# Where the last group step hands over to the first expert block: routing steps and two sums move behind the first block's preparation

## The chip, the cores and the metric

The kernel runs on one core of a Trainium2 chip. The metric is the device time of one execution in microseconds (us): the median of three runs for each kernel. One more execution was recorded by the hardware profiler, and all rows below are from that one.

The engines named here: PE is TensorE (matrix multiplies), DVE is VectorE, ACT is ScalarE, POOL is GpSimd (here mostly a scatterer of rows), and SP is SyncE, which issues most of the transfers. Each engine takes its instructions in the order in which the program wrote them.

## What is computed

First a long convolution per channel by a Fourier transform, then a mixture of experts with two levels of routing, each token going to one of 16 experts:

```
def reference(**kwargs):
    x = _attn_ref(x, h).reshape(8 * 5056, 128)   # irfft(rfft(x) * rfft(h)), 8 batches
    return _moe_ref(x, ...)

def _moe_ref(x, w_group, w_expert, w1, w2):      # 40448 tokens, 128 features
    g_idx = argmax(x @ w_group); g_w = softmax(x @ w_group)[g_idx]       # 4 groups
    e_idx = argmax(x @ w_expert[g]); e_w = softmax(...)[e_idx]           # 4 experts in each
    out[token] = g_w * e_w * (relu(x @ w1[g, e]) @ w2[g, e])             # 128 -> 1024 -> 128
```

## The kernel before

**Rounds.** The convolution is done in three rounds `r` of three sequences each (round 0: the filter and two batches). A round has `stage1(r)`, which transforms along one axis into the tile `st`; then `groups(r)`, which takes the 79 frequencies as 40 pairs `p` (`NQ` is 40; the last pair holds one frequency); then `side(r)`, which finishes the inverse transform, computes the routing of each unit of tokens and scatters the token rows, sorted by expert, into a table in memory (`srt`). `side(r)` runs beside the next round's work, and `side(1)` ends, with its eighth unit, at the place that is changed here. After round 2's groups come the expert blocks `j` of 512 tokens each; `side(2)` runs beside them.

**A group step** `step(k)` (L635) handles two pairs, `k` and `k+1`. It is a generator in eleven parts. In order: the forward transform of pair `k` on PE, its products `y` and `m` on DVE (L540), the same for pair `k+1`; then for both pairs the sum `y += m` (`add`, L572 to L576, on DVE in rounds 1 and 2), with one scatter sent between (`send`); then the inverse transforms on PE of the two pairs before, `k-2` and `k-1` (`inverse`, L578), each followed by a copy `zs` on ACT (L600, or L598 once the experts have begun) and a scatter sent by ACT. So the last full step, `k = 38`, sums pairs 38 and 39 and inverts 36 and 37. Pairs 38 and 39 are inverted by one more step, `k = 40`, whose eleven parts are the list `rest = late(2)` and are woven between the first expert steps, four parts ahead of each: part 1 stores pairs 36 and 37, part 3 inverts pair 38, part 4 pair 39, part 8 stores both. Parts 0 to 3 come ahead of the first expert step, part 4 ahead of the second.

**The hand-over.** After step 38 the entry `turn` (L1625) closes the PSUM pool of the groups (`pp`, three tiles of two banks, used in turn) and opens the experts' pool over the same banks (`pz`, `ptr1`, `px` twice, `ptr0`, `aux`; in this order, so `ptr0` and `aux` lie on the third pair of banks). Then `ffn_first(0)` (L1472) prepares block 0: `ffn_prep_x` transposes the token rows on PE into `ptr0` (L1306), copies ids on DVE (L1307, L1308), and splits x into a high part on ACT (`x0h`, L1298) and a low part on DVE (`x0l`, L1299); `ffn_prep_w` splits two quarters of the weights the same way (`w0h`, `w0l`, `w2h`, `w2l`).

**Expert steps.** A block has eight steps (`ffn_steps`, L1478). Step `i` does three matmuls of the first layer (`mm1`, L1351 to L1353) into one of three banks in turn, then ACT's `h..h` (L1356) and DVE's `h..l` (L1357), and from step 2 the second layer's three matmuls for step `i-2` (`mm2`, L1369 to L1371). Step 0 of block 0 also prepares `w1`, step 2 `w3`. From the fourth step on, a chain of small DVE instructions, `table_a`, computes which experts the blocks from 4 on take (L1097 and what follows); near its start stands one matmul (L1014, in `nblocks`) that needs the DVE instructions ahead of it and waits on PE in the order of the program.

**The routing steps.** Each unit of `side(1)` has 41 small steps, `gate_math` (L879), numbered 0 to 40 here, of which some are empty. Those that matter: 19 to 23 write weights and ids to the rows; 24 to 31 are empty; 32 is four small matmuls (L972, L973) into the bank that `routed()` gives, which is a tile of the groups' pool until the experts begin and the separate bank `py0` after that; 33 is `off` and `base` on DVE (L976, L977), 34 and 35 are `cs` (L979, L981), 36 and 37 `posf` (L984, L986); then a last step puts the unit's 15 scatters into the queue `sends`. `send` takes one scatter from the queue if there is one: DVE or ACT casts one column of positions (L854) and POOL issues the scatter (L855). What is left of the queue is sent at once at `drain`, after expert step 15. The load of block 4's rows (`ffn_x`, L1254 on SP) waits for all of these scatters.

**What sets the order.** All of this is one list `main` of (weight, function), and `weave` (L176) runs the side's steps between its entries:

```
        s["acc"] += w / s["len"]
        while s["done"] < len(s["steps"]) and (s["sacc"] < s["acc"] * s["total"] - 1e-6 or i == s["end"] - 1):
            sw, sf, small = s["steps"][s["done"]]
            if small and room[i + 1] > 0 and i < s["end"] - 1:
                light.append(sf)
            else:
                if small:
                    flush(len(light))
                sf()
```

A side step becomes due when the weights of the entries so far have reached its share. A small one (all of `gate_math`) is put in a waiting list, and the list is spread evenly over the run of entries of weight 0 that follows (`room` counts them; `if w == 0: flush(-(-len(light) // room[i]))`). In a group step the parts 6 and 10 weigh 2.0 and the others 0 (`GW`).

Of the kernel before, what the change touches and what calls it, by code (L numbers as in the profile page):

```python
# [44 lines left out]
NROW = 4  # L45
GW = [0, 0, 0, 0, 0, 0, 2.0, 0, 0, 0, 2.0]
FW = [0, 0, 1.0, 0, 0, 0, 1.0, 0]
W_S1, W_END = 0.45, 2.5
SIDE0, SIDE1, SIDE2 = 10, 14, 24
SLOTS = 56  # L50
LATE = 4
# [25 lines left out]
NQ = (NG + 1) // 2  # L77
# [153 lines left out]
class Kernel:  # L231
# [233 lines left out]
    def groups(self, r):  # L465
# [7 lines left out]
        w = nu * D  # L473
# [15 lines left out]
        def load_h(p):  # L489
            if p >= NQ:  # L490
                return
            ht = cx.tile([128, 3, D], F32, name="hg", bufs=3)
            if r > 0:
                nc.sync.dma_start(out=ht[:, 1:3], in_=self.hd[p])
            hgs[p] = ht

        def negate(p):
            if p < NQ:
                minus[p] = cx.tile([128, 128], F32, name="ns", bufs=2)
                nc.scalar.mul(out=minus[p], in_=cgs[p][:, 128:256], mul=-1.0)  # L500
# [113 lines left out]
        def loads(n):  # L614
            while asked[0] < n:
                load(asked[0])
                asked[0] += 1

        def limit(n):
            return min(n, max(n - 2, last_x + 2)) if r > 0 else n  # L620
# [14 lines left out]
        def step(k):  # L635


            last = [p for p in (k - 4, k - 3) if 0 <= p < NQ and r > 0]
            yield
            if k < NQ:  # L640
                self.beside = "groups"
            elif r < 2:
                self.beside = ""
            loads(limit(k + ahead + 1))
            load_h(k + 2)
            if k == 0:
                negate(0)
                negate(1)
            for p in (k, k + 1):
                if p < NQ:  # L650
                    yield from product(p)
                    if r == 0:
                        nc.sync.dma_start(out=self.hd[p], in_=hgs[p][:, 1:3])
                if p == k:
                    loads(limit(k + ahead + 2))
                    for q in last:
                        store(q)
            for p in (k, k + 1):
                if p < NQ:
                    add(p)  # L660
                    if p == k:
                        self.send()
            yield
            load_h(k + 3)
            back = [p for p in (k - 2, k - 1) if 0 <= p < NQ]
            for i in range(2):
                negate(k + 2 + i)
                if k - 2 + i in back:
                    yield
                    inverse(k - 2 + i)  # L670
                    if r == 2 or i == 1:
                        self.send("s")
            yield
            for _ in range(3 if k >= NQ else 0):
                yield
            if k >= NQ or r == 0:
                for p in back:
                    store(p)
            yield
# [921 lines left out]
    def run(self):  # L1601
        tc = self.tc
        with ExitStack() as ctx:
            self.pools(ctx)
            with ExitStack() as c2:
# [10 lines left out]
                def add(f, w=0.0):  # L1616
                    main.append((w, f))
# [17 lines left out]
                for r in range(3):  # L1635
                    if r == 1:
                        add(self.share)
                    pre, steps = gr[r]
                    rest = late(r - 1) if r > 0 else []
                    n = len(s1[r][1])  # L1640
                    t0 = self.table_0()
                    for k, f in enumerate(s1[r][1]):
                        add(f, W_S1)
                        if r > 0 and k % 2 == 1:
                            add(self.send)
                        if r == 0:
                            add(advance(more))
                        if r == 2 and ("end", 0) in mark:
                            add(advance(t0))
                        if k >= 1:  # L1650
                            for g in rest[RP * k - RP:RP * k]:
                                add(g)
                        if k == SIDE0 and r > 0:
                            add(side[r - 1][0])
                        if k == max(SIDE0 + SIDEG, END0 if r == 2 else 0) and r > 0:
                            mark["start", r - 1] = len(main)
                            if r == 2:
                                mark["end", 0] = len(main)
                        if k >= n - PRE and (k - n) % 5 == 0:
                            add(advance(pre))  # L1660
                    if r > 0:
                        add(lambda: None, W_END)
                    for p in range(0, NQ, 2):
                        for w, f in steps[p // 2]:
                            add(f, w)
                        if p >= NQ - LOAD1:
                            add(advance(s1[r + 1][0] if r < 2 else early))
                add(turn)
                add(lambda: self.ffn_first(0))
                rest = late(2)  # L1670
                ta, tq, tb, fill = self.table_a(), self.table_c(), self.table_b(), self.fill_rows()
                ahead = self.ffn_ahead()
# [69 lines left out]
```

## Time and profile before

| what | us |
|---|---|
| median of three runs | 1768.18 |
| lowest and highest of the three | 1767.53, 1774.45 |
| the profiled execution | 1765.39 |
| its span, first to last instruction | 1763.7 |

The profiled execution lies 2.79 us under the median, and 1.69 us of it lie outside its span. All places in this document are us from the start of that span. A busy time is the time in which an engine had at least one instruction running. In a line of a timeline the first number is the start and the second the time that the instructions took; DVE and ACT overlap the end of one with the start of the next, so that the distance of two starts is shorter than a duration. The brackets at the end give the idle time ahead of the line and what ended it.

### The profile page before, as it was taken

To read this page: it belongs to the slowest core of one execution; us is meant where nothing else is said; L and a number is where in the kernel's file an instruction comes from. 1 tells how busy PE (TensorE), PEld (TensorE's weight loads), DVE (VectorE), ACT (ScalarE), POOL (GpSimd) and SP (SyncE) were. 2 spreads that over 40 slices of the span, in tenths; PEclk is the share of its full clock that TensorE was granted. 3 is DMA by queue.
4 is the path that set the end of the run, shared out by engine and by line. 5 is a ranking of instruction groups with operands and counts; after the bars stand their busy time and mean duration, and the time that the engine had idled before them with its cause. 6 is when DMAs were issued, how large, how long until landed. Compare 5 with 4: busy or idle time off the path is not lost. (4 is left out here: it accounts for less than half of the span.)

```text
span 1763.7 us, 49283 instructions
## 1 busy us (share of the span) xinstructions
PE 1664.1 (94%) x17293; PEld 1289.9 (73%) x17293; DVE 1300.6 (74%) x3092; ACT 1041.4 (59%) x2461; POOL 769.3 (44%) x742
## 2 busy tenths in 40 slices
PE   8998899988898998999999999999999999999997
PEld 7676755557655556777777888787787877888986
DVE  6554598865487787777777778877787777877875
ACT  4564444434434445666666667676667666666765
POOL 1452233342355454144454445254555554334444
PEclk9999999999999999999999999999999999999998
DMA  7797578876578777655665555457545584444554
GB/s 204 217 294 222 163 237 250 263 224 182 167 228 256 252 229 213 175 161 166 172 176 165 165 150 152 126 158 234 161 147 157 170 248 140 130 130 145 156 163 144
DMA packets 281642, 330.30 MB, mean 187 GB/s; under 512 B 33335, under 2 KB 216000, under 8 KB 281368
## 3 DMA queue, kind: packets, MB, share of 16 engines
q1 hardware_dynamic: 252504, 271.00, 52.0%
q0 software_dynamic: 20608, 41.79, 6.9%
q10 hardware_dynamic: 8256, 14.10, 2.8%
q8 instruction: 143, 2.34, 0.6%
q14 instruction: 131, 1.07, 0.2%
HBM read 230.41 MB, written 96.86 MB: 186 GB/s over the span
## 5 line engine op out<-in xcount | busy, mean ns | idle before, releaser
L855 POOL DMA_INDIRECT srt<-rw,pos x320 | 345.8, 1081 | 446.7 <-DVE pos L854 129.3
L1422 POOL DMA_INDIRECT out<-orow,at x176 | 182.0, 1034 | 258.3 <-ACT at L1420 202.4
L540 DVE TENSOR_TENSOR y<-pp,hg 128x768 f32<-128x768 f32 (+1 forms) x120 | 103.6, 863 | 75.6 <-ACT hg L530 31.3
L1422 POOL DMA_INDIRECT out<-orow,sids x92 | 93.7, 1018 | 120.1 <-DVE orow L1389 86.8
L600 ACT COPY zs<-pp 128x768 f32<-128x768 f32 (+1 forms) x118 | 85.2, 722 | 85.9 <-PE pp L590 40.3
L590 PE MATMUL pp<-y,cg 64*64 64x384 f32 (+1 forms) x1472 | 117.2, 442 | 14.4 <-DVE m L540 11.1
L440 DVE TENSOR_TENSOR st<-pp,odd 128x320 f32<-128x320 f32 x96 | 46.9, 488 | 100.7 <-ACT odd L439 94.6
L522 PE MATMUL pp<-st,cg 64*64 64x192 f32 (+1 forms) x1556 | 116.9, 403 | 1.1 <-issue 1.1
L722 PE MATMUL py<-ig,zm 126*64 126x79 f32 x2048 | 93.7, 241 | 20.7 <-issue 14.0
L1357 DVE SCALAR_TENSOR_TENSOR h0l<-px,h0h 128x512 fp32r<-128x512 f32 (+1 forms) x109 | 73.5, 674 | 51.9 <-ACT h0h L1356 33.1
L722 PEld LDWEIGHTS py<-ig,zm 126*64 126x64 f32 x2048 | 80.6, 141 | 41.1 <-issue 29.0
L1356 ACT ACTIVATE h0h<-px 128x512 fp32r<-128x512 f32 (+1 forms) x109 | 63.9, 586 | 75.7 <-PE px L1353 47.7
L743 ACT COPY yT<-py 128x474 f32<-128x474 f32 (+1 forms) x96 | 44.6, 513 | 105.8 <-PE py L736 88.3
L540 DVE TENSOR_TENSOR m<-pp,hg 128x768 f32<-128x768 f32 (+1 forms) x120 | 102.8, 857 | 0.2
L1357 DVE SCALAR_TENSOR_TENSOR h2l<-px,h2h 128x512 fp32r<-128x512 f32 (+1 forms) x112 | 75.4, 673 | 34.8 <-ACT h2h L1356 25.2
L590 PEld LDWEIGHTS pp<-y,cg 64*64 64x64 f32 x1472 | 57.2, 133 | 53.9 <-issue 25.1
L1357 DVE SCALAR_TENSOR_TENSOR h3l<-px,h3h 128x512 fp32r<-128x512 f32 (+1 forms) x111 | 74.5, 671 | 29.3 <-ACT h3h L1356 27.2
L522 PEld LDWEIGHTS pp<-st,cg 64*64 64x64 f32 x1556 | 62.3, 133 | 39.7 <-issue 34.7
L1356 ACT ACTIVATE h3h<-px 128x512 fp32r<-128x512 f32 (+1 forms) x111 | 65.2, 587 | 37.9 <-PE px L1353 26.2
L574 POOL TENSOR_TENSOR y<-y,m 128x512 f32<-128x512 f32 x40 | 50.9, 1276 | 78.5 <-DVE m L562 46.1
L1357 DVE SCALAR_TENSOR_TENSOR h1l<-px,h1h 128x512 fp32r<-128x512 f32 (+1 forms) x111 | 74.6, 672 | 10.5 <-ACT h1h L1356 4.7
L1356 ACT ACTIVATE h1h<-px 128x512 fp32r<-128x512 f32 (+1 forms) x111 | 65.1, 587 | 24.2 <-PE px L1353 10.5
(476 smaller groups left out, 5184.6 us busy)
## 6 DMA issues: line engine op xcount, KB each, us to landing
wr<-in_moe_w SPq DMA_DIRECT2D x373, 256.0 KB
zd<-zs SPq DMA_DIRECT2D x78, 384.0 KB
zm<-zd SPq DMA_DIRECT2D x64, 378.0 KB
cg<-in_c_g SPq DMA_DIRECT2D x102, 224.0 KB
xr<-srt SPq DMA_DIRECT2D x71, 260.0 KB
hg<-hd SPq DMA_DIRECT2D x80, 128.0 KB
zd<-zs SPq DMA_DIRECT2D x39, 256.0 KB
xt<-in_x ACTq DMA_DIRECT2D x54, 160.0 KB
```

Of the source, the lines that this page charges most:

```text
L440: nc.vector.tensor_tensor(out=all_st[:, 0:2 * HALF, d], in0=even, in1=odd, op=ALU.add)
L522: nc.tensor.matmul(px[c * 64:c * 64 + 64, b, to], lhsT=k, rhs=data[:, of], start=begin, stop=i == len(steps) - 1 or p == 0 and i == 1, til ...
L540: nc.vector.tensor_tensor(out=t[:, :, 0:w].rearrange("p t (r u d) -> p t r u d", r=2, u=nu), in0=taken(px, part).unsqueeze(1).broadcast_to ...
L574: (nc.gpsimd if r == 0 else nc.vector).tensor_tensor(out=y[:, :, 0:w], in0=y[:, :, 0:w], in1=m[:, :, 0:w], op=ALU.add)
L590: nc.tensor.matmul(pz[c][h:h + 64, 0:w], lhsT=wt[c * 64:c * 64 + 64, k + h:k + h + 64], rhs=y[c * 64:c * 64 + 64, part, 0:w], start=part = ...
L600: nc.scalar.copy(out=z[:, 0:n, 0:w], in_=pp[:, 0:n, 0:w])
L722: nc.tensor.matmul(pys[q][c:c + 64, col(n, u)], lhsT=zms[q][:, n % QB, k:k + 64], rhs=self.ig[:, 0:NH], start=n % QB == 0 and u == 0, stop ...
L743: nc.scalar.copy(out=self.yT[:, k:k + QB * c1], in_=pys.pop(q)[:, 0:QB * c1])
L855: ins = self.nc.gpsimd.indirect_dma_start(out=self.srt, out_offset=bass.IndirectOffsetOnAxis(ap=k["pos"][0:p, j:j + 1], axis=0), in_=k["rw ...
L1356: nc.scalar.activation(out=hh, in_=p, func=AF.Relu)
L1357: nc.vector.scalar_tensor_tensor(out=hl, in0=p, scalar=0.0, in1=hh.bitcast(F32), op0=ALU.max, op1=ALU.subtract)
L1422: ins = self.nc.gpsimd.indirect_dma_start(out=self.a["out"], out_offset=bass.IndirectOffsetOnAxis(ap=ids, axis=0), in_=o, in_offset=None, ...
```

## The change

Three edits, all of which act in round 2 alone. The `add` of step 38 is left out, and with it the scatter that was sent there; step 40 now does both sums, in its part 1, which stands behind `ffn_first(0)`. The eleven parts of step 38 get the weight 1e-6 in place of 2.0 or 0. `ffn_first(0)` gets the weight that they had together, 4.0.

```
+W_S1, W_END, QUIET = 0.45, 2.5, 1e-6
             for p in (k, k + 1):
-                if p < NQ:
+                if p < NQ and (r < 2 or k < NQ - 2):
                     add(p)
                     if p == k:
                         self.send()
+                elif r == 2 and p >= NQ:
+                    add(p - 2)
             yield
...
                         for w, f in steps[p // 2]:
-                            add(f, w)
+                            add(f, w if r < 2 or p < NQ - 2 else QUIET)
...
                 add(turn)
-                add(lambda: self.ffn_first(0))
+                add(lambda: self.ffn_first(0), sum(GW))
```

## Rows read from the trace of the kernel before

**Rows 1.** The page, busy time and share of the span of two engines, and instructions.

```profile
PE 1664.1 (94%) x17293; PEld 1289.9 (73%) x17293; DVE 1300.6 (74%) x3092; ACT 1041.4 (59%) x2461; POOL 769.3 (44%) x742
```

**Rows 2.** Stretches of the hand-over: length, then busy us (and instructions) of PE, PE's weight loads, DVE, ACT and POOL, the granted clock of TensorE as a share of 2.4 GHz, the share of the transfer engines, GB/s.

```profile
662.00:669.00 7.00, 2.42 (x27) 1.13 (x24) 6.72 (x19) 2.01 (x5) 4.29 (x4) 1.00 0.72 210
669.00:678.00 9.00, 7.98 (x45) 4.37 (x44) 6.93 (x18) 6.71 (x17) 5.76 (x6) 1.00 0.85 259
678.00:695.00 17.00, 16.51 (x78) 13.20 (x78) 15.13 (x51) 10.98 (x26) 6.89 (x8) 1.00 0.65 171
```

**Rows 3.** The timeline of PE at the hand-over: the inverse of pair 37, the routing matmul, the transposes of block 0, the inverse of pair 38 (first matmul), the first expert step, the inverse of pair 39, the second expert step, the third (first matmul), and the matmul of `table_a`.

```profile
664.79 1.52 PE L590 MATMUL pp<-y,cg 64*64 64x384 f32 x16 [2.48 <-DVE m L540]
666.50 0.18 PE L972 MATMUL pp<-tot,ltri 128*128 128x16 bf16 x1 [0.18 <-DVE m L540]
...
668.67 0.63 PE L1306 MATMUL ptr<-ident,xr 128*128 128x128 f32 x4 [1.92 <-DVE base L977]
669.23 0.53 PE L590 MATMUL pz<-y,xt 64*64 64x384 f32 x1
...
670.68 0.50 PE L1351 MATMUL px<-x0h,w0h 128*128 128x512 f32 x1
671.49 0.50 PE L1352 MATMUL px<-x0h,w0l 128*128 128x512 f32 x1 [0.31 <-DVE w0l L1299]
...
672.15 1.51 PE L590 MATMUL pz<-y,xt 64*64 64x384 f32 x8
673.59 0.50 PE L1351 MATMUL aux<-x0h,w0h 128*128 128x512 f32 x1
...
674.39 0.40 PE L1351 MATMUL px<-x0h,w0h 128*128 128x512 f32 x1
...
678.11 0.17 PE L1014 MATMUL py<-nba_m,ones 128*128 128x16 bf16 x1 [0.82 <-DVE cnta L1099]
```

**Rows 4.** The timeline of DVE at the hand-over (of the two sums the first; the second, and one cast, stand between it and `off`).

```profile
665.49 0.95 DVE L540 TENSOR_TENSOR m<-pp,hg 128x768 f32<-128x768 f32 x1
666.35 0.95 DVE L574 TENSOR_TENSOR y<-y,m 128x768 f32<-128x768 f32 x1
...
668.15 0.17 DVE L976 TENSOR_TENSOR off<-pp,base 128x16 f32<-128x16 f32 x1
668.35 0.17 DVE L977 TENSOR_TENSOR base<-pp,base 128x16 f32<-128x16 f32 x1
...
670.01 0.38 DVE L1307 CAST ids<-xr 128x4 int32<-128x4 f32 x1
...
670.15 0.68 DVE L1299 TENSOR_TENSOR x0l<-ptr,x0h 128x512 fp32r<-128x512 f32 x1
...
671.35 0.68 DVE L1299 TENSOR_TENSOR w2l<-xt,w2h 128x512 fp32r<-128x512 f32 x1
672.89 0.69 DVE L1357 SCALAR_TENSOR_TENSOR h0l<-px,h0h 128x512 fp32r<-128x512 f32 x1 [0.85 <-ACT h0h L1356]
673.50 0.68 DVE L1299 TENSOR_TENSOR w1l<-xt,w1h 128x512 fp32r<-128x512 f32 x1
675.22 0.69 DVE L1357 SCALAR_TENSOR_TENSOR h1l<-aux,h1h 128x512 fp32r<-128x512 f32 x1 [1.04 <-ACT h1h L1356]
...
677.12 0.17 DVE L1097 TENSOR_TENSOR cnta<-base,base 128x16 f32<-128x16 f32 x1
```

**Rows 5.** The timeline of ACT at the hand-over: the copy of pair 37, the high part of x (no instruction stands between the two), and the first `h`.

```profile
666.42 0.80 ACT L600 COPY zs<-pp 128x768 f32<-128x768 f32 x1 [1.73 <-issue]
669.38 0.58 ACT L1298 CAST x0h<-ptr 128x512 fp32r<-128x512 f32 x1 [2.17 <-PE ptr L1306]
...
672.26 0.60 ACT L1356 ACTIVATE h0h<-px 128x512 fp32r<-128x512 f32 x1 [0.41 <-PE px L1353]
```

**Rows 6.** Two places where TensorE's granted clock fell, each with the idle stretch ahead of it and the stretch at the lower clock, and the two idle stretches of the hand-over. Columns as in the second group.

```profile
357.00:359.60 2.60, 0.00 (x0) 0.00 (x0) 2.57 (x7) 0.59 (x3) 1.34 (x2) 1.00 0.99 329
359.60:363.00 3.40, 3.37 (x48) 3.16 (x52) 0.59 (x6) 1.88 (x5) 1.64 (x2) 0.50 0.99 341
...
1250.40:1252.50 2.10, 0.05 (x2) 0.04 (x1) 0.54 (x1) 1.16 (x4) 0.00 (x0) 1.00 0.45 156
...
1253.90:1257.30 3.40, 3.40 (x10) 2.64 (x9) 2.19 (x6) 1.67 (x5) 2.09 (x2) 0.50 0.10 39
...
662.30:664.80 2.50, 0.02 (x2) 0.04 (x1) 2.42 (x8) 0.92 (x3) 1.53 (x2) 1.00 0.30 98
...
666.30:668.60 2.30, 0.27 (x7) 0.17 (x4) 2.27 (x7) 0.80 (x1) 1.49 (x2) 1.00 0.86 262
```

**Rows 7.** The drain and what waits for it: DVE's casts, the first and the last of POOL's four scatters, SP's load of block 4's rows, PE's transposes of these rows.

```profile
701.71 0.33 DVE L854 CAST pos<-posf 128x1 int32<-128x1 f32 x4
702.49 0.69 DVE L1357 SCALAR_TENSOR_TENSOR h0l<-aux,h0h 128x512 fp32r<-128x512 f32 x1 [0.45 <-issue]
...
702.13 0.98 POOL L855 DMA_INDIRECT srt<-rw,pos  x1 [4.23 <-DVE pos L854]
...
706.22 1.17 POOL L855 DMA_INDIRECT srt<-rw,pos  x1 [0.31 <-issue]
...
709.22 0.37 SPq L1254 DMA_DIRECT2D xr<-srt  x1
...
727.85 0.60 PE L1306 MATMUL ptr<-ident,xr 128*128 128x128 f32 x4
```

More of the change, by code (lines that the diff above doesn't have):

```diff
@@ L47 @@
 FW = [0, 0, 1.0, 0, 0, 0, 1.0, 0]
-W_S1, W_END = 0.45, 2.5
+W_S1, W_END, QUIET = 0.45, 2.5, 1e-6
 SIDE0, SIDE1, SIDE2 = 10, 14, 24
```

## The prediction, made before the changed kernel ran

> **What bounds the kernel now.** The page first: PE is busy 94% of the span and no other engine comes near [rows 1], so a change is worth what it takes from PE's idle time or adds to it. The place is the hand-over from the groups to the experts; the stretches around it show where PE's idle time lies. From 662 to 669 PE works 2.42 of 7 us while DVE works 6.72: that stretch is DVE's. From 669 to 678 PE works 7.98 of 9, and from 678 on 16.51 of 17 [rows 2]. So whatever moves the start of the busy stretch moves the end of the kernel by as much, and all that can be won here is the idle time of these 16 us, 5.6 us, or 3.2 us of it behind the inverse of pair 37, ahead of which nothing is moved that takes time. The timeline of PE names the waits behind it: 0.18, 1.92, 0.31 and 0.82 us [rows 3], 3.2 us in all. The largest, 1.92 us, is the transposes of block 0 waiting for `base`: the routing matmuls of the last unit take the third pair of PSUM banks, on which `ptr0` lies after `turn`, and DVE reads them only behind the two sums [rows 3, 4].
>
> **What moves.** I followed the weights through the list by hand. The last group step now has no entry of weight 0, so routing steps 19 to 27, which were spread up to the middle of that step, all come just ahead of it; 24 to 27 are empty, and of the others only 22 and 23 (0.1 to 0.2 us of DVE) pass from inside the step to its front, which shifts nothing behind pair 38's products. Steps 28 to 40 become due behind `ffn_first(0)` and are spread over the entries from `late` part 0 on: the four routing matmuls (32) land ahead of expert step 0, in bank `py0`; `off` and `base` behind expert step 0, the two `cs` and the two `posf` between it and expert step 1. The 15 scatters enter the queue behind the send of expert step 1. The two sums land in `late` part 1, behind block 0's low parts and ahead of the inverse of pair 38.
>
> **Step 1, the front: a gain of 2.07 us at the transposes.** Without the routing matmuls the third pair of banks is free when `m` of pair 39 ends, at 665.49 + 0.95 = 666.44; with the 0.15 us that lay between the end of `base` (668.52) and the transposes, they start at 666.6 in place of 668.67 [rows 3, 4]. The wait may be for the whole pool and so for the copy of pair 37, which ends at 667.22 [rows 5]: then 667.4. I take 666.6, since the wait of before also ended with one tile of that pair of banks; the other end, 0.8 us later, is kept for the range. `x0h` followed the start of the transposes by 0.71 us and `x0l` can follow `x0h` by 0.65: `x0h` 667.3, `x0l` 668.0, in place of 670.15 [rows 4, 5].
>
> **Step 2, what takes the place of the wait.** DVE takes its instructions in order, and behind `m` of pair 39 now stand the ids, `x0l`, `w0l`, `w2l`, and only then the sums. DVE idles from 666.6 to 668.0, where before it did the sums. `w2l` starts 1.20 us behind `x0l` and the next instruction could start 0.60 later: 669.8. The sums start there, the first ends after 0.95, at 670.75 (both took 1.8 us to the next instruction, 666.35 to 668.15 [rows 4], so they are over at 671.6), and the inverse of pair 38 starts at 670.9, in place of 669.23: 1.65 us late. PE idles from 667.2, where the transposes end, to 670.9: 3.7 us.
>
> **Step 3, expert step 0.** The inverse of pair 38 takes 1.45 us from start to next start (669.23 to 670.68), to 672.35. The routing matmuls add some 0.1. The first layer's three matmuls no longer wait for `w0l` (0.31 us): at 0.27 us each (673.59 to 674.39 for three) they run 672.45 to 673.25, and the last ends some 0.1 later [rows 3]. ACT has pair 38's two copies behind the inverse, over at about 673.3; so `h0h` starts at about 673.4, in place of 672.26, and `h0l`, which came 0.63 us later, at 674.0, in place of 672.89 [rows 4, 5]: 1.1 us late.
>
> **Step 4, the routing steps in the experts' way.** Behind `h0l` stand `w1l` (0.61 us later) and now the six routing instructions, which took from 668.15 to 670.01, 1.86 us [rows 4]. `w1l` starts at 674.6, the routing at 675.2, `h1l` at 677.1 in place of 675.22: 1.9 us late. Before, DVE idled 1.04 us ahead of `h1l`, so it is not all new time. PE does not mind at once: the inverse of pair 39 and expert steps 1 to 3 fill it to about 678.2. But `table_a`'s matmul L1014 stands in PE's order, its DVE instructions stand behind `h1l`, `h2l` and `w3l`, and it came 2.89 us behind the start of `h1l` [rows 3, 4]. It now comes at 680.0 in place of 678.11. Nothing behind it in the 17 us that follow has more than 0.5 us of idle time on PE [rows 2], so the 1.9 us stay.
>
> **Step 5, the scatters.** Before, the 15 scatters of the last unit went out at the two late inverses, at expert steps 0, 1, 2, 7, 8, 9 and 10 and at two stores in block 1, 11 in all, and 4 at the drain [rows 7]. Now the queue is empty at the first four of these places (before, ACT already found it empty at the inverse of pair 37: nothing stands between that copy and `x0h` [rows 5]; the send that is left out was the one that it can now use). So the drain has 8. DVE pays four more casts, some 0.33 us, against 0.45 us of idle time behind the four of before. POOL pays 4 x 1.36 us (706.22 - 702.13 over three), 5.5 us, and SP's load of block 4's rows, with block 4's weights behind it and then the next reads of the convolution's result, goes from 709.2 to 716.6 (5.5 and the 1.9 of above). PE wants those rows at 727.85 [rows 7], now 729.7: 13 us are left for the transfer. I cost it at nothing.
>
> **The clock.** Two rows show TensorE's clock falling from 2.4 to 1.2 GHz behind an idle stretch: after 2.6 us without a matmul at 357, and after 2.1 us at 1250.4; each time the lower clock held for the 3.4 us that the row covers. But 2.5 us of idle time at 662.3 and 2.3 us with little work at 666.3 passed at 2.4 GHz [rows 6], so idle time of this length goes either way. The 3.7 us of step 2 are longer than any of these, and follow close on 662.3's. The price: work of 3.4 us at half speed is 1.7 us late; what counts is only the part ahead of expert step 0's `h0h`, 670.9 to 673.3, for DVE has slack behind it. If the fall comes as PE resumes, the 2.4 us of work lose all 1.7; if it comes 1.4 us later, as it did at 1253.9 behind the matmuls that resumed at 1252.5, they lose 1.0 [rows 6]. The Trainium skill (TensorE: Matmul & The Clock Gate, section "Why this matters for your kernels") tells to keep idle gaps out from between bursts of matmuls, since such a gap brings TensorE back to the lower clock; this trace agrees at 357 and not at 662.3. By that rule the clock falls for certain; by the rows alone it is likely.
>
> **The sum.** Gained: nothing that lasts. Lost: 1.9 us by steps 2 to 4, and 1.0 to 1.7 us if the clock falls; I take 1.0, since the rows have falls that came later than the first matmul. 1765.39 + 2.9 = 1768.3 us for a profiled execution, and 1768.18 + 2.9 = 1771.1 us on the median, 0.16%. A measurement of this kernel can tell some 0.5%, 9 us, from no change: this is the same within it.
>
> **The rivals.**
> *The late steps without the clock* (0.25): all of the above and no fall: 1770.1.
> *It does what it looks like* (0.20): PE starts block 0 two us sooner and the sums and routing hide beside PE. For it: DVE idled 0.85 us ahead of `h0l` and 1.04 ahead of `h1l` [rows 4], room for the 1.86 us of routing. Against it: DVE's order puts the sums behind `x0h`'s round trip, and the inverse of pair 38 stands ahead of expert step 0 on PE. At best all 3.2 us of waits go: 1765.0; if step 2 alone fails, some 1768, no change at all.
> *The drain decides, clearly slower* (0.05): block 4's rows, loaded from 716.6, reach PE after 729.7, and PE waits. No row here shows how long this load takes; of before it can be said that it took no more than 727.85 - 709.22 = 18.6 us, since PE has no wait there [rows 7]. It decides from a load of 13.1 us on; with one of 18.6 PE waits 5.5 us: 1768.18 + 1.9 + 5.5 = 1775.6, and with a fall of the clock at its highest price 1777.3, which is beyond the 0.5%. Against it: block 4's weights come behind it in the same queue and were in time too, and a load of 260 KB (512 rows of 130 numbers) is 1.5 us even at the 171 GB/s that all transfers had behind 678 [rows 2].
>
> **Chances and range.** The forecast with the fall has 0.46, with 1771.1 to 1772.6 as its own range (a fall at 1.7 us and the 0.8 us of step 1 on top); the rest as given, and 0.04 for what I have not seen that makes it faster by over 0.5%. The three cases within 0.5% have 0.91 together, slower 0.05, faster 0.04. The three runs of before lie from 0.65 under their median to 6.27 above, and the profiled execution 2.79 under it, so a median can move by 2 to 4 us by itself: from 1765.0, the best of the gains, to 1776, the forecast with most of that spread on top.
>
> **What the profile would show.** Right: transposes at about 666.6 (step 1); sums behind `w2l` and the inverse of pair 38 near 670.9 (step 2); `h0l` near 674.0 (step 3); six routing instructions between `w1l` and `h1l` and L1014 near 680 (step 4; half to one and a half us later with a fallen clock); 8 casts at the drain, and the load of block 4's rows near 716 to 717 with no wait on PE for it (step 5); and a granted clock of 0.5 between 669 and 675. Wrong: the inverse of pair 38 before 669.5, L1014 before 678, or a wait of PE's past 690 that the trace of before does not have.

## The result, and the profile after

The changed kernel is slower: a median of 1783.26 us over 8 runs against 1771.68 for the kernel before in 8 runs beside it, a ratio of 1.0067 with an interval of 1.0046 to 1.0088. The forecast was 1771.1, no change within 0.5%; of the 12.2 us between it and the measured median 3.5 are the kernel before's own, which took 1768.18 then. The profiled execution took 1793.08 us, with a span of 1791.4, 27.7 us more than the profiled one of before. That is more than the medians differ. 10.8 us of it lie ahead of the changed place, in code that the two kernels share (`m` of pair 39 starts at 676.25 in place of 665.49), where the clock fell oftener in this execution (mean granted clock 0.977 over the span, 0.990 in that of before). They are left aside. Places are therefore given from the start of that `m`, and three stretches are compared:

| stretch | before | after |
|---|---|---|
| `m` of pair 39 to `table_a`'s matmul (the hand-over) | 12.62 | 19.18 |
| `table_a`'s matmul to the transposes of block 4's rows | 49.74 | 57.21 |
| from there to the start of PE's last matmul | 1029.55 | 1032.45 |

So the changed kernel loses 6.6 us at the hand-over and 7.5 us in the stretch with the drain. The last row differs by up to 6.6 us among the runs of one sitting below, whose code is the same there (1029.91 to 1036.49 in the third), so its 2.9 us are not put down to the change. Lines of the code after are two higher than before (L1306 is L1308, L1014 is L1016).

PE's timeline at the hand-over after, which answers to [rows 3]:

```profile
678.02 0.66 PE L1308 MATMUL ptr<-ident,xr 128*128 128x128 f32 x4 [0.95 <-ACT zs L600]
682.19 0.90 PE L590 MATMUL pz<-y,xt 64*64 64x384 f32 x1 [3.51 <-DVE y L574]
...
685.10 0.77 PE L1353 MATMUL px<-x0h,w0h 128*128 128x512 f32 x1
...
686.65 2.83 PE L590 MATMUL pz<-y,xt 64*64 64x384 f32 x8
689.41 0.79 PE L1353 MATMUL aux<-x0h,w0h 128*128 128x512 f32 x1
...
695.43 0.18 PE L1016 MATMUL py<-nba_m,ones 128*128 128x16 bf16 x1
```

The transposes come 1.78 us behind `m`, where they came 3.18 behind it. The inverse of pair 38 comes 5.94 behind it, where it came 3.74, and PE is idle for 3.51 us ahead of it. The durations show the rest: 2.83 us for the inverse of pair 39 against 1.51, 0.77 for a first-layer matmul against 0.50. PE runs at half its clock, as three stretches of after show (columns as in [rows 2]):

```profile
678.70:681.10 2.40, 0.00 (x0) 0.00 (x0) 1.72 (x3) 1.62 (x3) 1.18 (x2) 1.00 0.76 217
681.10:694.80 13.70, 12.61 (x44) 6.74 (x45) 7.33 (x17) 4.24 (x9) 0.96 (x1) 0.50 0.47 144
694.80:706.00 11.20, 10.83 (x50) 8.23 (x49) 9.67 (x37) 7.22 (x16) 2.32 (x3) 1.00 0.67 194
```

It stays at 1.2 GHz for 13.7 us. The longest that [rows 6] showed was 3.4. PE is idle only in the first 1.1 of the 13.7 us, ahead of the inverse of pair 38; behind that the profile shows it busy without a pause:

```profile
682.20:694.80 12.60, 12.60 (x44) 6.73 (x45) 6.24 (x15) 4.24 (x9) 0.96 (x1) 0.50 0.44 136
```

DVE's timeline after, which answers to [rows 4]:

```profile
679.38 0.69 DVE L1301 TENSOR_TENSOR x0l<-ptr,x0h 128x512 fp32r<-128x512 f32 x1 [1.80 <-issue]
...
680.59 0.69 DVE L1301 TENSOR_TENSOR w2l<-xt,w2h 128x512 fp32r<-128x512 f32 x1
681.19 1.82 DVE L574 TENSOR_TENSOR y<-y,m 128x768 f32<-128x768 f32 x2
687.39 0.69 DVE L1359 SCALAR_TENSOR_TENSOR h0l<-px,h0h 128x512 fp32r<-128x512 f32 x1 [4.38 <-ACT h0h L1358]
688.00 0.68 DVE L1301 TENSOR_TENSOR w1l<-xt,w1h 128x512 fp32r<-128x512 f32 x1
688.60 0.17 DVE L978 TENSOR_TENSOR off<-py,base 128x16 f32<-128x16 f32 x1
...
690.36 0.17 DVE L988 TENSOR_TENSOR posf<-posf,sg 128x15 f32<-128x15 f32 x1
691.72 0.69 DVE L1359 SCALAR_TENSOR_TENSOR h1l<-aux,h1h 128x512 fp32r<-128x512 f32 x1 [1.18 <-ACT h1h L1358]
```

The order is the predicted one. But DVE still waits 1.18 us for `h1h` behind the six routing instructions: with the clock low they cost nothing, and PE is what is late.

The drain after, which answers to [rows 7]: DVE's casts, POOL's first and last scatter, SP's load of block 4's rows, PE's transposes of these rows.

```profile
719.16 0.57 DVE L856 CAST pos<-posf 128x1 int32<-128x1 f32 x8
...
719.58 0.98 POOL L857 DMA_INDIRECT srt<-rw,pos  x1 [4.51 <-DVE pos L856]
...
728.92 1.01 POOL L857 DMA_INDIRECT srt<-rw,pos  x1 [0.31 <-issue]
...
731.45 0.37 SPq L1256 DMA_DIRECT2D xr<-srt  x1
...
752.64 0.60 PE L1308 MATMUL ptr<-ident,xr 128*128 128x128 f32 x4
```

PE does not wait for these rows. But what PE does while POOL scatters is another matter. `side(2)` gives PE, now and then, a lump of 72 small matmuls (48 of L724, 24 of L738; L722 and L736 before). PE's timeline of the one beside the drain, after:

```profile
722.58 1.73 PE L724 MATMUL py<-ig,zm 126*64 126x79 f32 x44
724.64 0.38 PE L724 MATMUL py<-ig,zm 126*64 126x79 f32 x4 [0.33 <-issue]
725.40 0.50 PE L738 MATMUL py<-igt,zt 64*64 64x158 f32 x5 [0.37 <-issue]
726.83 0.54 PE L738 MATMUL py<-igt,zt 64*64 64x158 f32 x5 [0.94 <-issue]
728.28 0.50 PE L738 MATMUL py<-igt,zt 64*64 64x158 f32 x5 [0.91 <-issue]
729.72 1.16 PE L738 MATMUL py<-igt,zt 64*64 64x158 f32 x5 [0.94 <-issue]
731.17 0.81 PE L738 MATMUL py<-igt,zt 64*64 64x158 f32 x4 [0.29 <-issue]
```

The same lump in before, with two scatters beside it, and the next one, with none:

```profile
705.15 1.85 PE L722 MATMUL py<-ig,zm 126*64 126x79 f32 x47
707.22 0.23 PE L722 MATMUL py<-ig,zm 126*64 126x79 f32 x1 [0.21 <-issue]
707.38 1.62 PE L736 MATMUL py<-igt,zt 64*64 64x158 f32 x24
...
736.06 1.86 PE L722 MATMUL py<-ig,zm 126*64 126x79 f32 x48
737.85 1.04 PE L736 MATMUL py<-igt,zt 64*64 64x158 f32 x24
```

Of these three the one with no scatter takes 2.83 us, the one with two 3.85 and the one with six 9.39. In the last, PE stops after the first 44 matmuls and then after every four or five, for 0.3 to 0.9 us, and waits for nothing that the profile names. Two scatters have no fixed price: other lumps of before with two beside them took 2.83 to 6.15 us. Meanwhile the transfer engines are at 16% and DVE works 1.29 of 9.5 us, so neither looks like the bound (the last four columns are the busy POOL, the clock, the transfer share and GB/s):

```profile
722.50:732.00 9.50, 5.72 (x74) 3.47 (x74) 1.29 (x2) 1.14 (x3) 5.91 (x6) 0.84 0.16 50
728.90:735.70 6.80, 5.70 (x20) 3.85 (x21) 1.39 (x2) 1.77 (x4) 1.43 (x2) 0.50 0.43 130
```

At 728.9 the clock falls once more, for 6.8 us. The lump is 5.5 us longer than that of before; the other 2 of the 7.5 us are put down to this low clock, which no run shows apart from a long lump.

### The profile page after: what moved, and what is told of

The parts are those of the page before. It is cut to its first block, busy times and chain, and to the rows that moved or that the text cites. A ratio compares the mean times of both kernels' runs of the same rounds, so it can differ in the third digit from the quotient of the medians.

```text
span 1791.4 us, 49283 instructions
## 1 busy us (share of the span) xinstructions
PE 1682.0 (94%) x17293; PEld 1297.5 (72%) x17293; DVE 1303.5 (73%) x3095; ACT 1042.9 (58%) x2458; POOL 767.5 (43%) x742
## 5 line engine op out<-in xcount | busy, mean ns | idle before, releaser
L724 PE MATMUL py<-ig,zm 126*64 126x79 f32 x2048 | 92.0, 238 | 20.0 <-issue 14.2
L724 PEld LDWEIGHTS py<-ig,zm 126*64 126x64 f32 x2048 | 79.4, 139 | 41.5 <-issue 29.6
L1359 DVE SCALAR_TENSOR_TENSOR h1l<-px,h1h 128x512 fp32r<-128x512 f32 (+1 forms) x111 | 74.7, 673 | 16.2 <-ACT h1h L1358 11.6
```

What stands on the lines that cost most here:

```text
L724: nc.tensor.matmul(pys[q][c:c + 64, col(n, u)], lhsT=zms[q][:, n % QB, k:k + 64], rhs=self.ig[:, 0:NH], start=n % QB == 0 and u == 0, stop ...
L1359: nc.vector.scalar_tensor_tensor(out=hl, in0=p, scalar=0.0, in1=hh.bitcast(F32), op0=ALU.max, op1=ALU.subtract)
```

## The experiments

The experiments ran in four sittings, each beside the kernel before on the same chip. In the first two the kernel before took 1697.48 and 1694.32 us, in the others 1772.79 and 1758.43. One chip served in the second and in the last, so this is no property of a chip. In the first two, the short sittings, the lump at the drain takes 2.83 us (in one run 3.00) with two or three scatters beside it, but for the run in which it was moved. The page's group of L722 shows the difference over the whole kernel, in before and, below it, in the kernel before of the second sitting (busy time, mean ns, idle time ahead and what ended most of it):

```profile
L722 PE MATMUL py<-ig,zm 126*64 126x79 f32 x2048 | 93.7, 241 | 20.7 <-issue 14.0
```

```profile
L722 PE MATMUL py<-ig,zm 126*64 126x79 f32 x2048 | 82.6, 236 | 9.4 <-ACT rw L780 5.4
```

The 14.0 us of idle time without a named releaser no longer lead. So the short sittings show the hand-over alone, the long ones both costs.

**The first sitting: one part at a time.** Sums put back in the changed kernel (weights kept):

```
-                if p < NQ and (r < 2 or k < NQ - 2):
+                if p < NQ:
                     add(p)
...
-                elif r == 2 and p >= NQ:
-                    add(p - 2)
```

> The changed kernel with its first edit undone: the sums of pairs 38 and 39 and the scatter between them are back in the last group step; the weights stay, so the routing steps stay behind block 0's preparation. From the start of pair 39's product m to table_a's matmul it was 12.62 us before and 19.18 after; from that matmul to block 4's transposes 49.74 before and 57.21 after. Theory (PE's idle gap in front of the inverse of pair 38 lets the clock fall, and apart from that the doubled drain holds up the side's matmuls): the first stretch comes back to 11.5 to 14 us with no fall of the clock in it, the second stays long, 54 to 58 us, since the drain still has 8 scatters. Rival (the routing steps between h0l and h1l are what costs): the first stretch stays at 16 us or more.

The second is the kernel before with this edit the other way round. The third is the changed kernel with sends at all of the first eight expert steps, the fourth the kernel before with the sends of its first four places left out (two at the late inverses, two at expert steps 0 and 1):

```
-                    elif k < 8 * (NA - 2) and k % 8 not in (3, 4, 5, 6):
+                    elif k < 8 * (NA - 2) and (k % 8 not in (3, 4, 5, 6) or k < 8):
...
-                    if r == 2 or i == 1:
+                    if k < NQ and (r == 2 or i == 1) or r < 2 and i == 1:
...
-                    elif k < 8 * (NA - 2) and k % 8 not in (3, 4, 5, 6):
+                    elif 1 < k < 8 * (NA - 2) and k % 8 not in (3, 4, 5, 6):
```

> The kernel before with the first edit alone: the sums move behind block 0's preparation, the routing steps and the queue of scatters stay as they were. Theory: the gap in front of the inverse of pair 38 is shorter than after the whole change, since the transposes wait for base again (base comes 1.8 us earlier without the sums ahead of it, the transposes at some 1.4 us behind m of pair 39); the first stretch 13.5 to 17 us, the upper end if the clock falls; the drain has 4 scatters and the second stretch is 49 to 51 us. Rival (the sums are harmless, the routing steps cost all of it): first stretch 12.6 us or less. Rival (the second stretch is long for another reason than the drain): 54 us or more.

> The changed kernel with a scatter sent at four more expert steps, 3 to 6 of block 0, so that the drain has 4 again in place of 8. Theory (scatters that run beside the side's small matmuls hold them up): the second stretch falls from 57.2 to 49 to 52 us, the first stays near 19 us or wherever the clock puts it (14.5 to 20), and the median comes some 5 to 7 us under the changed kernel's 1783. Rival (the second stretch is long because of the clock or of loads that came late): it stays at 54 us or more, since only the order of 4 scatters differs.

> The kernel before with the four sends at the two late inverses and at expert steps 0 and 1 left out, so that the drain has 8 scatters; nothing else is moved. Theory: the first stretch stays at 12 to 13 us; the side's second unit of 72 matmuls, 3.85 us before and 9.39 after, takes 8 to 10 us, and the second stretch 54 to 58 us; the median some 5 to 8 us above before. Rival (a long drain costs nothing by itself): 49 to 51 us.

Measured, with what the second and third sitting add (the hand-over; the stretch to block 4; the time at 1.2 GHz that began within 2 us ahead of the hand-over or in it):

| kernel | ratio, interval | hand-over | to block 4 | low |
|---|---|---|---|---|
| sums put back | 0.9987, 0.9967 to 1.0007 | 11.67 | 47.56 | 0 |
| sums moved only | 1.0005, 0.9986 to 1.0025 | 17.89 | 47.68 | 3.4 + 6.8 |
| changed, drain of 4 | 1.0014, 0.9991 to 1.0037 | 19.02 | 47.58 | 13.7 |
| before, drain of 8 | 0.9994, 0.9967 to 1.0021 | 13.61 | 47.48 | 3.4 |
| *second sitting:* changed | 1.0053, 1.0031 to 1.0076 | 20.74 | 47.56 | 20.5 |
| before | 1.0015, 0.9998 to 1.0031 | 12.62 | 47.50 | 3.4 |
| changed, filler of 8 | 1.0036, 1.0019 to 1.0053 | 18.23 | 47.57 | 0 |
| changed, lump later | 1.0126, 1.0108 to 1.0143 | 16.93 | 58.11 | 6.8 |
| *third sitting:* changed, filler of 4 | 1.0038, 1.0019 to 1.0056 | 16.47 | 55.12 | 3.4 |
| sums back, drain of 0 | 1.0016, 0.9990 to 1.0041 | 11.68 | 54.32 | 0 |
| before, drain of 8 | 1.0026, 1.0012 to 1.0041 | 12.64 | 57.47 | 3.4 |
| before, drain of 0 | 0.9995, 0.9979 to 1.0010 | 13.97 | 49.72 | 6.8 |

Moving the sums makes the hand-over longer by itself, and putting them back makes it 1 us shorter than before: the late routing of the weights is no loss. The timed ratios of the second and third kernel are smaller than their 5.3 and 6.4 us at the hand-over (0.31% and 0.38%) would make them; one profiled execution does not tell how long the clock stays low in the others, and that of the second kernel was the slowest of its ten runs. The drain costs nothing here, with 8 scatters too: the 54 to 58 us expected of the first and the fourth kernel did not come.

**The second sitting.** The two kernels of the comparison again:

> The changed kernel itself once more, since the four experiments before ran beside a kernel before of 1697 us and not of 1772. Theory (the fall of the clock in the hand-over belongs to the change, the hold-up of the side's matmuls beside the drain belongs to executions in which these matmuls are slow to issue): from pair 39's m to table_a's matmul 17 to 20 us with a fall of the clock of 7 us or more; the side's second unit of 72 matmuls takes 2.8 to 3 us where the kernel before takes that for its own, and 8 to 10 us where the kernel before takes 3.5 us or more. Median 1 to 5 us above before in the first case, 8 to 14 in the second. Rival (the drain costs in any case): the unit takes 8 us or more also beside a kernel before of 1697 us.

> The kernel before itself once more, for its trace in the same conditions as the three others of this call. Both theories: a median equal to that of the kernel before beside it; pair 39's m to table_a's matmul 12.0 to 14.5 us, the upper end with a single fall of the clock of 3.4 us; from there to block 4's transposes 47.5 us where the side's units take 2.8 us, 49 to 51 where they take 3.5 or more.

and the changed kernel with eight matmuls that nobody reads, issued behind `ffn_first(0)` to fill PE's idle time, and with the side's lumps four expert steps later:

```
+        for _ in range(8):
+            self.nc.tensor.matmul(t, lhsT=self.ident, rhs=self.yT[:, 0:512], start=True, stop=True)
...
-START2 = 14
+START2 = 18
```

> The changed kernel with eight matmuls of 512 columns put between block 0's preparation and the late steps, on data that nothing else uses and into a bank that nobody reads: they leave the computation as it is and only keep PE at work in the gap ahead of the inverse of pair 38, some 3 to 4 us. Theory (the gap brings the clock down, and the low clock is most of the delay): the clock stays at 2.4 GHz in the hand-over or falls for 3.4 us at most, and pair 39's m to table_a's matmul takes 14 to 16 us in place of 19.1. Rival (the order on DVE is the delay, the clock only goes with it): 18 us or more, filler or not.

> The changed kernel with the first units of the side that runs beside the experts starting four expert steps later, at step 18 in place of 14, so that its units stand behind the drain, which comes after step 15, by more than the eight scatters take. Theory: where the kernel before has slow units (3.5 us or more), the second unit comes back from 9 us to under 5, and from table_a's matmul to block 4's transposes it is 45 to 52 us; where the units take 2.8 us in any case, nothing is won but what the later start moves out of this stretch. Rival (late loads hold the unit): it stays long.

The filler took 7.03 us and was too long for its place: the inverse of pair 38 came 9.23 us behind `m` in place of 5.94. So the 18.23 us at its hand-over, the number that the rival named, do not decide between the two; the chain behind the filler does. For the filler kept the clock up. Its stretches (columns as in [rows 2]), the filler first and then the inverse of pair 38 to `table_a`'s matmul:

```profile
618.95:625.90 6.95, 6.95 (x18) 2.86 (x16) 3.63 (x5) 1.62 (x3) 1.36 (x2) 1.00 0.65 191
625.90:634.90 9.00, 7.57 (x47) 4.41 (x47) 5.81 (x16) 4.83 (x11) 2.09 (x2) 1.00 0.38 126
```

The second takes 8.99 us at the full clock, and 13.24 in after (682.19 to 695.43): the low clock costs 4.25 us there. 5.94 + 8.99 = 14.93 us is, as an estimate from these two runs, what the hand-over of the changed kernel would take without it.

The later lump failed, and showed something else. The first lump now came beside the drain and the second close behind it, and both waited for their input; PE's row for the second, and SP's queue:

```profile
677.69 3.43 PE L724 MATMUL py<-ig,zm 126*64 126x79 f32 x48 [7.54 <-DMA zm<-zd]
```

```profile
667.46 0.37 SPq L1256 DMA_DIRECT2D xr<-srt  x1
...
671.00 0.46 SPq L706 DMA_DIRECT2D zm<-zd  x1
...
673.34 6.55 SPq L706 DMA_DIRECT2D zm<-zd  x2
```

The load of block 4's rows waits for the drain at the head of SP's queue, 9.8 us for the scatters, and the second lump's loads stand behind it. Read so, the drain can hold up PE in this way too, in a short sitting; the changed kernel's own lump comes too early for it.

**The third sitting.** The filler with `range(4)`; the sums put back and sends at the first sixteen steps (`or k < 16`); and the kernel before with eight scatters left for the drain, and with none (`or k < 8`).

> The changed kernel with four extra matmuls of 512 columns (nobody reads their result) that TensorE runs in its idle time behind the first sums of the hand-over. Eight of them took 7.03 us and pushed the inverse of pair 38 back by 3.3 us; four should take about 3.5 us and fit the 3.5 us in which TensorE waited for y, so that the inverse stays near 5.9 to 6.5 us behind the m of pair 39. Theory (the hand-over's excess over the forecast is the low clock): no long stretch at 1.2 GHz, inverse of pair 38 to the matmul of table a about 9 us as in the run with eight, the matmul of table a 14.5 to 16 us behind the m of pair 39, and the time 1 to 4 us under that of the changed kernel, still 2 to 4 us more than with the sums put back. Rival (the order of the steps sets it, not the clock): 18 us or more with the clock high throughout.

> The changed kernel's late routing of the weights kept, its sums put back where the kernel before has them, and the routing's sends given steps enough that none is left for the drain. Theory: the hand-over as with the sums put back alone (11 to 12.5 us against 12.6 in the kernel before) and no scatter beside the side's second unit of small matmuls, which then takes 2.8 to 3.0 us on any chip. Where scatters lengthen that unit (the kernel before at about 1770 us), 2 to 4 us faster than the kernel before; where they do not (1695 us), 0 to 2 us faster. Rival: the additional sends among the expert's steps cost DVE and GpSimd time there, and the stretch from the matmul of table a to block 4's transposes grows over 49 us.

> The kernel before with its first four sends left for the drain: eight scatters there instead of four, nothing else changed. Theory: where the kernel before takes about 1770 us beside it, the side's unit beside the scatters takes 6 to 9.5 us instead of 3.85 and the stretch from the matmul of table a to block 4's transposes grows from 49.7 us to 53 to 57; where it takes about 1695 us, the unit takes 2.8 us and nothing changes, as in the first run of this kernel. Rival: the stretch stays at 49.7 us on the slower chip too, and the changed kernel's 57.2 us had another cause.

> The kernel before with sends at four more of the expert's steps, so that the drain has no scatter left; nothing else changed. Theory: the side's unit takes 2.8 us on any chip; where the kernel before takes about 1770 us this saves 1 us of the 49.7 us between the matmul of table a and block 4's transposes, where it takes about 1695 us nothing. Rival: the scatters among the expert's steps slow those steps themselves, and the stretch is longer by 1 us or more.

The four-matmul filler took 3.6 us; from the inverse of pair 38 on it again took 8.99 us, here with the inverse no later behind the transposes than in after (4.18 us, there 4.17):

```profile
674.58 0.53 PE L590 MATMUL pz<-y,xt 64*64 64x384 f32 x1
...
683.57 0.17 PE L1016 MATMUL py<-nba_m,ones 128*128 128x16 bf16 x1 [1.44 <-DVE nba_m L1011]
```

The fall that this execution does show began 0.8 us ahead of the hand-over and the transposes came 1.5 us later than in after; that is why 16.47 stands there and not the 14.5 to 16 expected.

Eight scatters in the otherwise unchanged kernel before make the stretch 57.47 us, as in the changed kernel (57.21). PE's timeline of the lump:

```profile
707.92 0.40 PE L722 MATMUL py<-ig,zm 126*64 126x79 f32 x5 [0.38 <-issue]
708.70 0.49 PE L736 MATMUL py<-igt,zt 64*64 64x158 f32 x5 [0.37 <-issue]
710.15 0.48 PE L736 MATMUL py<-igt,zt 64*64 64x158 f32 x4 [0.96 <-issue]
711.59 0.49 PE L736 MATMUL py<-igt,zt 64*64 64x158 f32 x4 [0.96 <-issue]
```

It took 9.48 us. With no drain left (before, drain of 0) it took 2.83, but the stretch stayed at 49.72: PE now waits 0.84 us ahead of a second-layer matmul at 694.31, amid the scatters that were moved ahead, a wait that before does not have. In the sums-back kernel the sends at all of the first sixteen steps left nothing for the drain, but five scatters (one of them of finished rows, L1422) met the first lump, which took 9.01 us in place of 4.04; my expectation that no scatter would be beside a lump was wrong. ACT makes the casts there, so DVE's casts are not the cause.

**The last sitting: the square.** Both undone (sums back and sends at the first eight steps), either alone, neither:

> The changed kernel with only its late routing of the weights kept: the two sums are put back, and four more sends among the expert's first steps leave the drain four scatters as in the kernel before. Theory (two causes that add up): hand-over 11.7 us against 12.6 in the kernel before, the matmul of table a to block 4's transposes 49.5 to 50 us, so 1 us faster than the kernel before at most, a ratio of 0.998 to 1.001. Rival (a third cost of the change that neither repair removes): 1.003 or more where the kernel before takes about 1770 us.

> The changed kernel with its sums put back, the drain of eight scatters kept. Theory: where the kernel before takes about 1770 us beside it, hand-over 11.7 us, the side's unit beside the scatters 8 to 9.5 us and the matmul of table a to block 4's transposes 55 to 57.5 us: 4 to 7 us slower than the kernel before, a ratio of 1.002 to 1.004. Where it takes about 1695 us, as in the first run of this kernel: 0 to 3 us faster. Rival (the drain's cost needs the low clock of the hand-over ahead of it): 50 us and no slower than the kernel before on either chip.

> The changed kernel with its sums left where it has them and the drain brought back to four scatters. Theory: hand-over 16 to 20 us with a stretch of 7 to 21 us at 1.2 GHz, the matmul of table a to block 4's transposes 49.5 to 51 us: 4 to 8 us slower than the kernel before on any chip, a ratio of 1.002 to 1.005. Rival (the drain is the whole of it): no slower than the kernel before.

> The changed kernel as it is, beside the other three. Theory: hand-over 18 to 21 us and, where the kernel before takes about 1770 us, the matmul of table a to block 4's transposes 55 to 58 us: the excess over the kernel before is the sum of those of the other two kernels within 3 us, 9 to 14 us, a ratio of 1.005 to 1.008. Rival: the two overlap, and the excess is that of the larger alone.

| kernel | ratio, interval | hand-over | to block 4 | lump |
|---|---|---|---|---|
| both undone | 0.9989, 0.9970 to 1.0008 | 11.68 | 49.56 | 3.68 |
| sums back, drain of 8 | 1.0041, 1.0021 to 1.0061 | 11.67 | 57.63 | 9.17 |
| sums moved, drain of 4 | 1.0031, 1.0012 to 1.0050 | 20.73 | 49.58 | 3.73 |
| changed kernel | 1.0073, 1.0047 to 1.0098 | 18.72 | 57.34 | 9.16 |

Each cost is there by itself, and they add up: 0.42% + 0.52% over both undone, less the 0.11% that both undone lies under before, makes 1.0083, within the interval of 1.0073. The drain costs its 8 us with the clock high throughout the hand-over (in that run it falls at 704.8, 4.5 us into the lump), so it needs no low clock ahead of it. A third cost that neither repair removes does not show: both undone lies between 0.9970 and 1.0008. The version with both undone keeps the late routing and cannot be told from before (the forecast was 1 us faster at most). None of the runs beat the kernel before by more than the measurement can tell.

## Why the prediction was wrong

**Step 1** held at its other end. The transposes waited for ACT's copy, 0.95 us: the whole pool. They came at 1.78 us behind `m` where 1.1 was taken and 1.9 named as the late case.

**Step 2** held: sums behind `w2l`, the inverse of pair 38 at 5.94 us (5.41 by the sum, 0.67 lost in step 1), PE idle for 3.51 us (3.7).

**Steps 3 and 4** held as the chain without the clock: 14.93 us to `table_a`'s matmul, by the runs with filler, against the 680.0 - 665.49 = 14.5 of the sum. In the execution itself `h0l` came at 11.14 in place of 8.5, and L1016 at 19.18.

**The clock** was the right mechanism with the wrong size. A fall was forecast for the time at which PE resumes or later; it came 1.1 us ahead of that, at 681.1. Its price was put at 1.0 to 1.7 us, from rows that held the low clock for 3.4 us, and only for the work ahead of `h0h`, "for DVE has slack behind it". It held for 13.7 us and cost 4.25. The term that failed is the length: 3.4 us were taken over from the two places of [rows 6], and the low clock here lasted four times as long. Waits of PE's in between do not explain it, for behind 682.2 the profile shows none. Why the clock stayed low so long no run tells. Over all profiled executions, those with the sums in place show 0, 3.4 or 6.8 us at 1.2 GHz here, those with the sums moved 6.8 to 20.5, the two with a filler 0 and 3.4. Nor does the fall always belong to the new gap. In three of the seven executions with the sums moved and no filler it came 0.4 to 1.2 us ahead of `m`, and so it did in three of those with the sums in place or a filler. There it ended after 3.4 us; with the sums moved it lasted 20.5 us twice, and once came back 3.4 us later for 6.8. In these runs the change shows in how long the clock stays low, not in whether it falls. The Trainium skill (TensorE: Matmul & The Clock Gate, section "Why this matters for your kernels") tells to keep gaps out from between bursts; the trace agrees here, with 3.51 us of gap and a fall ahead of its end.

**Step 5** failed: "I cost it at nothing". It followed the scatters only to those who wait for their result: DVE's casts (0.57 us, right), the load of block 4's rows (55.2 us behind `m` against 51.1 by the sum, the hand-over's 4.7 us later), PE's transposes (no wait, right). It did not look at what runs beside them. The trace of before had the answer. Its lumps take 2.83 us with no scatter and up to 6.88 beside four; this is that one, on PE (the clock was at 1.2 GHz from 567.8 to 571.2 and has a part in its length; the waits of 0.52 and 1.14 us began ahead of that):

```profile
564.81 0.69 PE L722 MATMUL py<-ig,zm 126*64 126x79 f32 x13 [1.30 <-issue]
565.66 0.23 PE L722 MATMUL py<-ig,zm 126*64 126x79 f32 x1
566.40 0.32 PE L722 MATMUL py<-ig,zm 126*64 126x79 f32 x2 [0.52 <-issue]
567.86 2.39 PE L722 MATMUL py<-ig,zm 126*64 126x79 f32 x32 [1.14 <-issue]
570.18 1.51 PE L736 MATMUL py<-igt,zt 64*64 64x158 f32 x24
```

This step carries 7.5 us of the loss. In a short sitting it would have held (47.56 us of the changed kernel against 47.50 of before); here it did not.

**The rivals.** The case that ended on the right side, "the drain decides, clearly slower", had the right place and a wrong mechanism: block 4's rows came in time. It names SP's queue, and that is where the later lump lost 7.54 us; the changed kernel lost nothing there. The list of wrong signs held one that fired in kind: a wait of PE's past 690 that before has only in part, the gaps in the lump.

**The sum.** 2.9 us were forecast and 11.6 measured on the medians, 14.0 by the two stretches: 14.93 - 12.62 = 2.3 from steps 1 to 4, 4.25 from the clock, 7.5 from the drain. Of these the sum had 1.9, 1.0 and 0.

## What to carry to other kernels

Cost a moved transfer or scatter twice: by who waits for its result, and by what runs beside it in its new place; look up in the trace what that neighbour takes with and without such company. Price a new idle gap of TensorE by all the work that resumes behind it: here the low clock lasted through the whole chain, and not the 3.4 us that two other places of the trace had shown. And where two small costs fall under what a measurement can tell, read them by stretches between fixed landmarks in the profile, and repeat in another sitting before one is called harmless.

## What the runs showed of the hardware

Small matmuls in a dense row are held up, in some sittings, while POOL issues indirect transfers. In the ten traces with spans of 1758 to 1791 us, 69 of the 72 lumps of 72 matmuls that no scatter met took 2.83 or 2.84 us, and all 65 that met three or more took 3.05 to 9.48. A longer lump also meets more scatters, so the counts alone do not show the cause; the kernel before with eight scatters and with none at the drain does (9.48 and 2.83 us), with the transfer engines at 16% in after. In 117 of the 320 lumps of these traces PE's waits of over 0.1 us without a named releaser add up to more than 0.2 us, in the eight traces of the two short sittings in none of 256. One chip showed both. What PE lacks in those gaps the profile does not name, and no run here tells it. One transfer of the instruction queue q8 runs beside the lump of after (722.5 to 732) and one beside that of before (705 to 709), so the traces do not point at a late instruction either. Why whole sittings differ by 3.6 to 4.6% stays open too.

The clock, once at 1.2 GHz, stayed there for up to 20.5 us while PE worked 16.05 of these, in the run with the sums moved and a drain of four of the last sitting (columns as in [rows 2]); in the last 10.2 us of them it was busy without a pause:

```profile
664.80:685.30 20.50, 16.05 (x64) 8.19 (x57) 10.81 (x25) 6.75 (x14) 4.02 (x4) 0.50 0.50 161
685.30:695.00 9.70, 9.46 (x43) 7.08 (x42) 8.15 (x34) 6.82 (x17) 6.18 (x7) 1.00 0.86 240
```
